# Normalising pair 0 of an attention-and-mixer kernel in a tile of its own, and finishing the first norms on VectorE

## The chip, the cores and the metric

The kernel runs on one core of one Trainium2 chip. The metric is the device time of one launch in microseconds (us); lower is better. A core has TensorE (PE: matrix products and transposes, results in PSUM), VectorE (DVE), ScalarE (ACT), GpSimd (POOL), SyncE (SP, which here only issues transfers), and DMA engines that move data between memory and SBUF. Each engine works through its own list of instructions in order and waits on semaphores for the others.

## The reference

Cosine attention for 8 batches of 12 heads, 448 rows of 64 elements, followed by a mixer over the rows (tokens) and the 768 channels of each batch:

```python
q_n = q / (np.linalg.norm(q, axis=-1, keepdims=True) + 1e-06)
k_n = k / (np.linalg.norm(k, axis=-1, keepdims=True) + 1e-06)
scores = np.matmul(q_n, k_n.transpose(0, 1, 3, 2)) / tau
scores = scores - np.max(scores, axis=-1, keepdims=True)
attn = np.exp(scores)
attn = attn / (np.sum(attn, axis=-1, keepdims=True) + 1e-09)
x = np.matmul(attn, v)            # then heads side by side: [batch, 448, 768]

xt = x.transpose(0, 2, 1)
h = np.maximum(xt @ w_tok1, 0.0) @ w_tok2
u = x + h.transpose(0, 2, 1)
h2 = np.maximum(u @ w_ch1, 0.0) @ w_ch2
out = u + h2
```

`tau` is 0.1. The weights are 448x256, 256x448, 768x1536 and 1536x768.

## The kernel before

**Tiling.** The heads are taken two at a time: 48 pairs, six to a batch. Three pairs make a half batch `n`, whose q, k and v come in one transfer each. The 448 rows of a head are split into 384 main rows, three to each of 128 partitions (`qm`, `km`, `vm`), and 64 rest rows (`xq`, `xk`, `xv`). Rest rows of q lie on 64 partitions, all heads side by side; those of k and v lie on 128 partitions, the two heads of a pair above each other.

**Norms.** For each pair the kernel squares q and k (`squares`, L174 on ScalarE or L176 on VectorE or GpSimd), sums the squares of each row on VectorE (`sums`, L189), and turns sums into reciprocal norms (`rnorms`, L197 to L200: four small ScalarE activations, Ln, Exp with scale 0.5, Ln with the epsilon, Exp with scale -1). `scaled` (L207) multiplies k and q by the reciprocal norm and writes half-precision operands into `kqs`. The rest rows have the same steps, one call for the three pairs of a half batch: `squares_x`, `sums_x` (L193), `scaled_x` (L213 for q, L218 twice for k). Sums and reciprocal norms of a half batch lie in one tile of 45 columns: 0 to 8 for the rest rows, then 12 for each pair.

**A pair.** TensorE transposes the scaled operands into PSUM (`tpose`, L246, L247), VectorE copies them out (`qk_copy`, L251), TensorE computes the scores in three chunks and one for the rest rows (`score`, L266; `score_x`, L273), ScalarE takes the exponential of each (L267, L274), TensorE multiplies by v (`pv`, L287, L289), and VectorE divides by the row sums (L292, L293). `cast_v` brings v to half precision, its main rows on VectorE (L164, for the first two half batches) and its rest rows on GpSimd (L168). Then come the token mixer (L307, L326) and, one whole batch at a time, the channel mixer (L354, L368), whose units are fed between the steps of later pairs.

**Order.** The schedule is written out by hand: each engine runs its instructions in program order. A prologue issues the first loads, fills constants, and carries pair 0 through its norm, with the squares of pairs 1 and 2 placed between. Pair 0's norm runs in two pieces, one for its main rows and one for the rest rows of the whole half batch. `busy` (L232) issues matrix products of no use ahead of and between pair 0's transposes and ahead of the first scores. Then a loop over `i` takes pair `i` through its scores, prepares the norms of later pairs (dictionaries `rn_at`, `sq_at`, `sc_at` say at which `i`), and issues loads on SP's queue. In `i` = 0 GpSimd scales pair 1, issues the token weights on its own queue (L141, L142, L144), scales pair 2, and squares k of pair 3; at `i` = 1 VectorE sums pair 3 and the rest rows of its half batch, and ScalarE starts their norm.

Of the kernel before, what the change touches and what calls it, by code (L numbers as in the profile page):

```python
# [22 lines left out]
def kernel(  # L23
# [56 lines left out]
    sqx = cst.tile([P, 9, E], FP32, name="sqx")  # L80
    ssqs = [cst.tile([P, 45], FP32, name=f"ssq{i}") for i in range(3)]
# [29 lines left out]
    def load_v(n):  # L111
        nc.sync.dma_start(**main(vm, v, "vm", n, bufs=2))

# [69 lines left out]
    def squares_x(n, eq, ek):  # L183
        square(eq, sqx[0:XR, 0:6], xh(xq, n, 6))
        square(ek, sqx[:, 6:9], xh(xk, n, HP))

    def sums(p):
        lo = 9 + 12 * (p % HP)
        nc.vector.tensor_reduce(out=ssqs[p // HP % 3][:, lo:lo + 12],  # L189
                                in_=sq[p][:].rearrange("p a g e -> p (a g) e"), axis=AXX.X, op=ALU.add)  # L190
# [4 lines left out]
    def rnorms(n, c0=0, c1=45):  # L195
        ssq, rn = ssqs[n % 3][:, c0:c1], rns[n % 3][:, c0:c1]
        nc.scalar.activation(out=rn, in_=ssq, func=AF.Ln, bias=tiny[:])  # L197
        nc.scalar.activation(out=rn, in_=rn, func=AF.Exp, scale=0.5)
        nc.scalar.activation(out=rn, in_=rn, func=AF.Ln, bias=eps[:])
        nc.scalar.activation(out=rn, in_=rn, func=AF.Exp, scale=-1.0)  # L200

    def scaled(p, eng):
        n, j = p // HP, p % HP
        for a, src in enumerate((mh(km, p), mh(qm, p))):
            lo = 9 + 12 * j + 6 * (1 - a)
# [4 lines left out]
    def scaled_x(n, eng, j0=0, j1=HP):  # L210
        rn, kq = rns[n % 3], kqs[n % 2]
        gs = slice(2 * j0, 2 * j1)
        eng.tensor_tensor(out=kq[0:XR, j0:j1, 1, NC, :].rearrange("p j (g e) -> p j g e", g=2),  # L213
                          in0=xh(xq, n, 6)[:, gs].rearrange("p (j g) e -> p j g e", g=2),
                          in1=_bcast_free(rn[0:XR, gs].rearrange("p (j g) -> p j g", g=2), E), op=ALU.mult)
        for g in range(2):
            r = slice(XR * g, XR * (g + 1))
            eng.tensor_tensor(out=kq[r, j0:j1, 0, NC, E * g:E * g + E], in0=xh(xk, n, HP)[r, j0:j1],  # L218
                              in1=_bcast_free(rn[r, 6 + j0:6 + j1], E), op=ALU.mult)

# [16 lines left out]
    def tpose(p):  # L237
        n, j = p // HP, p % HP
        pst = ps.tile([P, 8 * P], FP16, name=f"pst_{p}", tag="b")
        if p == 0:  # L240
            w = ps.tile([P, 512], FP32, name="busy", tag="b")
            busy(w, 26)
        for a, c in [(a, c) for a in range(2) for c in range(NC)] + [(0, NC)]:
            if p == 0 and (a, c) == (0, NC):
                busy(w, 4)
            nc.tensor.transpose(pst[:, P * (4 * a + c):P * (4 * a + c + 1)], kqs[n % 2][:, j, a, c], id16[:])  # L246
# [412 lines left out]
```

## Time and profile before

| | |
|---|---|
| median of 9 runs | 415.18 us (413.37 to 416.23) |
| the profiled execution | 413.37 us, of which 411.6 us is the span that the profile covers |
| TensorE busy | 390.7 us, 95% of the span |
| ScalarE | 226.5 us, 55% |
| GpSimd | 213.8 us, 52% |
| VectorE | 201.7 us, 49% |
| mean granted TensorE clock | 0.993 |

The page divides the span into 40 slices of 10.3 us, and gives for each the tenths in which an engine was busy. Further views give the busy time in any stretch, the instructions in order of time, what ended the idle time ahead of an instruction, and the chain of work that ended last. In the timeline a line gives start, duration, engine, line of the program, operation, output and input with shapes, and how many instructions were merged; in brackets stands the idle time before it and what ended that. Names of buffers are given without their numbers.

### The profile page before, as it was taken

Reading aid. Unit: us, or ns where it says so; the run is one execution under the profiler, and the core shown is the slowest. Engines: PE = TensorE matmul, PEld = TensorE weight load, DVE = VectorE, ACT = ScalarE, POOL = GpSimd, SP = SyncE. Lnnn points to the kernel's source line nnn. Section 1 sums busy time; section 2 is a strip of 40 time slices with the busy share of each in tenths; the row PEclk is TensorE's granted clock in tenths of the full one; section 3 lists DMA queues with packets and bytes.
Section 4 is the critical chain, followed back from the end, with each engine's and each line's share of the span. In section 5 each row is a group of like instructions: output and inputs, shape, how many; then the busy total and the mean of one; then the engine's idle time right before and its main releaser. Section 6 shows DMA issues by size and latency. Waiting matters only on the chain.

```text
span 411.6 us, 9121 instructions
## 1 busy us (share of the span) xinstructions
PE 390.7 (95%) x3650; PEld 226.2 (55%) x3650; DVE 201.7 (49%) x455; ACT 226.5 (55%) x405; POOL 213.8 (52%) x314
## 2 busy tenths in 40 slices
PE   8589788999999999999999999999999999999995
PEld 3256444666555655456555555555555565565562
DVE  5588535577543564446543555356553443233021
ACT  4788296974575546664566436664566434611400
POOL 3985669699076675849391937658582500000000
PEclk9989999999999999999999999999999999999998
DMA  7999999989796697969896497979893353013012
GB/s 214 284 241 195 182 244 225 233 201 235 149 224 87 168 196 167 245 127 251 187 246 111 122 222 168 233 115 242 188 184 49 98 136 65 15 53 102 2 76 76
DMA packets 137162, 67.51 MB, mean 164 GB/s; under 512 B 93152, under 2 KB 133536, under 8 KB 137120
## 3 DMA queue, kind: packets, MB, share of 16 engines
q1 hardware_dynamic: 132800, 61.46, 70.6%
q0 software_dynamic: 3632, 5.18, 7.5%
q8 instruction: 28, 0.46, 0.5%
q10 hardware_dynamic: 688, 0.30, 0.3%
q14 instruction: 14, 0.11, 0.1%
HBM read 43.38 MB, written 11.01 MB: 132 GB/s over the span
## 4 chain that ended last, share of the span: by engine, by line
PE 78%; POOL 8%; DVE 5%; issue 4%; ACT 3%; DMA 1%; POOLq 0%; DVEq 0%; ACTq 0%
PE psG L354 25%; PE psF L368 24%; PE psO L287 7%; PE psS L266 7%; PE psR L307 4%; PE psU L326 4%; POOL kq L207 3%; PE psX L273 3%; PE psO L289 2%; POOL sq L176 2%; POOL kq L218 1%; DVE ssq L189 1%; ACT pt L267 1%; DMA km<-in_k_dram 1%; PE psU L331 1%
## 5 line engine op out<-in xcount | busy, mean ns | idle before, releaser
L267 ACT ACTIVATE pt<-psS 128x896 f16<-128x896 f32 x144 | 126.4, 914 | 71.8 <-PE psS L266 71.8
L354 PE MATMUL psG<-ut,wc1t 128*128 128x448 f16 x576 | 122.2, 353 | 0.0
L368 PE MATMUL psF<-wc2t,gt 128*128 128x384 f16 x672 | 117.1, 326 | 0.0
L356 ACT ACTIVATE gt<-psG 128x448 f16<-128x448 f32 x96 | 52.1, 544 | 77.3 <-PE psG L354 77.2
L207 POOL TENSOR_TENSOR kq<-km,rn 128x384 f16<-128x384 f32 x47 | 39.1, 831 | 98.3 <-ACT rn L200 97.1
L368 PEld LDWEIGHTS <-gt 128*128 128x128 f16 x672 | 63.6, 98 | 40.2 <-issue 2.2
L354 PEld LDWEIGHTS <-wc1t 128*128 128x128 f16 x576 | 52.5, 98 | 47.4 <-issue 5.9
L371 DVE TENSOR_TENSOR ost<-psF,ur 128x384 f32<-128x384 f32 x56 | 31.2, 557 | 79.9 <-PE psF L368 78.0
L287 PEld LDWEIGHTS <-pt 128*128 128x128 f16 x1152 | 51.9, 98 | 16.3 <-issue 5.2
L287 PE MATMUL psO<-vt,pt 128*128 128x65 f16 x1152 | 58.0, 194 | 0.0
L189 DVE TENSOR_REDUCE ssq<-sq 128x12 f32<-128x768 f32 x48 | 45.1, 948 | 19.6 <-POOL sq L176 18.4
L266 PE MATMUL psS<-qk 64*128 64x448 f16 x288 | 44.8, 357 | 7.9 <-ACT pt L267 5.5
L176 POOL TENSOR_TENSOR sq<-km 128x384 f32<-128x384 f32 x47 | 39.0, 833 | 9.0 <-DMA km<-in_k_dram 5.6
L293 DVE TENSOR_TENSOR x<-psO,rec 128x256 f16<-128x256 f32 x96 | 40.8, 425 | 3.3
L289 PE MATMUL psO<-vx,pt 128*128 128x130 f16 x192 | 42.0, 219 | 0.0
L207 POOL TENSOR_TENSOR kq<-qm,rn 128x384 f16<-128x384 f32 x47 | 38.9, 828 | 0.0
L292 DVE RECIPROCAL rec<-psO 128x4 f32<-128x4 f32 x96 | 17.1, 178 | 44.5 <-PE psO L289 44.3
L266 PEld LDWEIGHTS <-qk 64*128 64x128 f16 x288 | 11.0, 94 | 38.7 <-issue 32.7
L326 PE MATMUL psU<-w2t,r 128*128 128x448 f16 x96 | 25.9, 353 | 4.2 <-DVE r L310 3.2
L307 PE MATMUL psR<-x,w1t 128*128 128x128 f16 x384 | 29.2, 219 | 0.0
L336 DVE TENSOR_TENSOR ut<-psU,xT 128x448 f16<-128x448 f32 (+2 forms) x39 | 17.6, 477 | 22.5 <-PE psU L326 15.0
L274 ACT ACTIVATE pt<-psX 128x448 f16<-128x448 f32 x48 | 26.0, 542 | 0.0
(62 smaller groups left out, 332.2 us busy)
## 6 DMA issues: line engine op xcount, KB each, us to landing
vm<-in_v_dram SPq DMA_DIRECT2D x16, 576.0 KB, 7.1
out_dram<-ost SPq DMA_DIRECT2D x24, 384.0 KB, 2.8
qm<-in_q_dram SPq DMA_DIRECT2D x15, 576.0 KB, 5.5
km<-in_k_dram SPq DMA_DIRECT2D x15, 576.0 KB, 7.2
wc1t<-in_moe_w_ch_dram POOLq DMA_DIRECT2D x2, 1152.0 KB, 13.5
wc2t<-in_moe_w_ch_dram POOLq DMA_DIRECT2D x2, 1152.0 KB, 12.0
out_dram<-ost SPq DMA_DIRECT2D x8, 192.0 KB, 2.8
xq<-in_q_dram SPq DMA_DIRECT2D x7, 192.0 KB, 7.9
```

Source lines behind the costliest of these rows:

```text
L176: eng.tensor_tensor(out=out, in0=src, in1=src, op=ALU.mult)
L189: nc.vector.tensor_reduce(out=ssqs[p // HP % 3][:, lo:lo + 12], in_=sq[p][:].rearrange("p a g e -> p (a g) e"), axis=AXX.X, op=ALU.add)
L207: eng.tensor_tensor(out=kqs[n % 2][:, j, a, 0:NC, :].rearrange("p c (g e) -> p g c e", g=2), in0=src, in1=_bcast_free(rn, E), op=ALU.mult)
L266: nc.tensor.matmul(psS[:, g, 0:S], qk[r, P * c:P * (c + 1)], qk[r, 512:512 + S], start=True, stop=True)
L267: nc.scalar.activation(out=pt[:, 2 * S * c:2 * S * (c + 1)].rearrange("p (g s) -> p g s", g=2), in_=psS[:, :, 0:S], func=AF.Exp, scale=inv ...
L287: nc.tensor.matmul(psO[:, mm, E1 * g:E1 * (g + 1)], pt[:, at:at + P], vt[:, 2 * j + g, c, 0:E1], start=(g == 0 and c == 0), stop=False)
L289: nc.tensor.matmul(psO[:, mm, :], pt[:, PX + lo:PX + lo + P], vx[:, j, 0:2 * E1], start=False, stop=True)
L307: nc.tensor.matmul(psR[:, tt, :], w1t[:, m, tt * P:(tt + 1) * P], xs[p][:, m, :], start=(m == 0), stop=(m == NC))
L326: nc.tensor.matmul(psU[:], rs[p][:, tt, :], w2t[:, tt, lo:lo + S], start=(tt == 0), stop=by_dma and tt == TT - 1)
L354: nc.tensor.matmul(psG[:], wc1t[:, dt, ct * P:(ct + 1) * P], ut[:, dt, sp], start=(dt == 0), stop=(dt == DT - 1))
L356: nc.scalar.activation(out=gt[:, ct, sp], in_=psG[:], func=AF.Relu)
L368: nc.tensor.matmul(psF[:], gt[:, ct, lo:lo + P], wc2t[:, ct, dh * DH:(dh + 1) * DH], start=(ct == 0), stop=(ct == CT - 1))
```

## The change

- Pair 0's q and k, main rows and rest rows, are loaded into one tile `own` that lies in a buffer of the later tile `ut16`: q as 2 heads of 4 rows (three main, one rest), k as 6 main columns and one rest column. The transfers are q main and q rest on SP, k main and twice k rest on ACT. The unused half of q's rest column is set to zero by VectorE.
- Pair 0 has sums and reciprocal norms of its own. ScalarE squares q, GpSimd k; VectorE reduces each.
- The norm of pairs 0, 1 and 2 is two ScalarE activations (Ln, Exp) and then an add of the epsilon and a reciprocal on VectorE. Pair 1 and the rest rows of pairs 1 and 2 go together; pair 2 follows. Later pairs keep the four activations.
- Pair 0's k is scaled and transposed first, then its q; ScalarE copies the k half out of PSUM and VectorE the q half. Squares of pair 1 and of the rest rows are issued between.
- Pair 1's q half and q's rest rows of pairs 1 and 2 are scaled by VectorE, the k halves by GpSimd; before, VectorE did pair 0's rest rows and GpSimd the others and all of pair 1. These stand in the loop, between the first two score chunks of pair 0, and with them the sum of pair 2.
- The cast of v's first half batch moves from the end of the prologue to behind the token weights' issue; pair 2's scaling follows it.
- The rest rows of k for pairs 1 and 2 are loaded through GpSimd's queue, those of q on SP's queue behind k's load.
- The filler products are 20 and 2 instead of 26 and 4.

```diff
+    own = mix.tile([P, 30, E], FP32, name="own", tag="ut16")
+    q0 = own[:, 0:8].rearrange("p (g c) e -> p g c e", g=2)
+    k0, sq0 = own[:, 8:15], own[:, 15:30]
+    ssq0 = cst.tile([P, 15], FP32, name="ssqp")
+    rn0 = cst.tile([P, 15], FP32, name="rnp")
...
+    def load_pair0():
+        nc.sync.dma_start(out=q0[:, :, 0:NC].rearrange("p g c e -> p g (c e)"),
+                          in_=q[0, 0:2, 0:SM].rearrange("g (p c) e -> p g (c e)", c=NC))
+        nc.scalar.dma_start(out=k0[:, 0:6].rearrange("p (g c) e -> p g (c e)", g=2),
+                            in_=k[0, 0:2, 0:SM].rearrange("g (p c) e -> p g (c e)", c=NC))
+        nc.sync.dma_start(out=q0[0:XR, :, NC], in_=q[0, 0:2, SM:S].rearrange("g p e -> p g e"))
+        for g in range(2):
+            nc.scalar.dma_start(out=k0[XR * g:XR * (g + 1), 6], in_=k[0, g, SM:S])
...
+    def rn_roots(ssq, rn):
         nc.scalar.activation(out=rn, in_=ssq, func=AF.Ln, bias=tiny[:])
         nc.scalar.activation(out=rn, in_=rn, func=AF.Exp, scale=0.5)
+
+    def rn_inverse(rn):
+        nc.vector.tensor_scalar_add(out=rn, in0=rn, scalar1=EPS_NORM)
+        nc.vector.reciprocal(out=rn, in_=rn)
...
+    def scaled_0(part):
+        kq = kqs[0][:, 0, part]
+        if part:
+            nc.vector.tensor_tensor(out=kq.rearrange("p c (g e) -> p g c e", g=2), in0=q0,
+                                    in1=_bcast_free(rn0[:, 0:8].rearrange("p (g c) -> p g c", g=2), E), op=ALU.mult)
+            return
+        nc.vector.tensor_tensor(out=kq[:, 0:NC].rearrange("p c (g e) -> p g c e", g=2),
+                                in0=k0[:, 0:6].rearrange("p (g c) e -> p g c e", g=2),
+                                in1=_bcast_free(rn0[:, 8:14].rearrange("p (g c) -> p g c", g=2), E), op=ALU.mult)
+        for g in range(2):
+            r = slice(XR * g, XR * (g + 1))
+            nc.vector.tensor_scalar_mul(out=kq[r, NC, E * g:E * g + E], in0=k0[r, 6], scalar1=rn0[r, 14:15])
...
-    rn_at = {0: [(0, 33, 45)]}
+    rn_at = {}
...
-        load_q(0, 0, 2)
-        load_k(0, 0, 2, nc.scalar)
-        load_xq(0, 0, 6)
-        load_xk(0, 0, 6, nc.scalar)
+        load_pair0()
         load_q(0, 2, 6)
...
         load_k(0, 2, 6)
+        load_xq(0, 2, 6)
         load_v(0)
...
+        nc.vector.memset(q0[XR:P, :, NC], 0.0)
...
                                 fill=1.0, base=0, pattern=[[-1, P]], channel_multiplier=1)
+        load_xk(0, 2, 6, nc.gpsimd)
...
-        squares(0, nc.scalar, nc.vector)
-        sums(0)
-        rnorms(0, 9, 21)
-        squares_x(0, nc.scalar, nc.vector)
+        w = ps.tile([P, 512], FP32, name="busy", tag="b")
+        busy(w, 20)
+        square(nc.scalar, sq0[:, 0:8], own[:, 0:8])
+        square(nc.gpsimd, sq0[:, 8:15], k0)
+        nc.vector.tensor_reduce(out=ssq0[:, 0:8], in_=sq0[:, 0:8], axis=AXX.X, op=ALU.add)
+        nc.vector.tensor_reduce(out=ssq0[:, 8:15], in_=sq0[:, 8:15], axis=AXX.X, op=ALU.add)
+        rn_roots(ssq0[:], rn0[:])
+        rn_inverse(rn0[:])
+        scaled_0(0)
+        pst = tpose(0, (0,))
         squares(1, nc.scalar, nc.gpsimd)
+        squares_x(0, nc.scalar, nc.gpsimd)
+        scaled_0(1)
+        tpose(0, (1,), pst)
+        nc.scalar.copy(out=qk_tile(0)[:, 0:P * 4], in_=pst[:, 0:P * 4])
+        nc.vector.tensor_copy(out=qks[0][:, P * 4:P * 7 + XR], in_=pst[:, P * 4:P * 7 + XR])
         sums_x(0)
-        scaled(0, nc.vector)
-        rnorms(0, 0, 9)
-        scaled_x(0, nc.vector, 0, 1)
         sums(1)
-        rnorms(0, 21, 33)
+        busy(w, 2)
         squares(2, nc.scalar, nc.gpsimd)
-        scaled_x(0, nc.gpsimd, 1, HP)
-        qk_copy(0, tpose(0))
-        sums(2)
-        cast_v(0)
...
                 score(i, 0, 2 if i < 4 else 0)
+                if i == 0:
+                    rn_roots(*rn_cols(0, 0, 21))
+                    rn_inverse(rn_cols(0, 0, 21)[1])
+                    scaled(1, nc.vector, (1,))
+                    scaled(1, nc.gpsimd, (0,))
+                    scaled_x(0, nc.vector, 1, HP, (1,))
+                    scaled_x(0, nc.gpsimd, 1, HP, (0,))
+                    sums(2)
                 score(i, 1)
...
             if i == 0:
-                scaled(1, nc.gpsimd)
                 weights_tok()
+                rn_roots(*rn_cols(0, 21, 33))
+                cast_v(0)
+                rn_inverse(rn_cols(0, 21, 33)[1])
                 scaled(2, nc.gpsimd)
```

`scaled`, `scaled_x` and `tpose` take a new argument that names the halves (0 for k, 1 for q). `squares_x(0)` leaves pair 0's rest rows out. In half batch 0 the 12 columns of pairs 1 and 2 stand at 9 and 21 (`col`), since pair 0 has its own.

## The prediction

> **What bounds the kernel now.** I read the page's slices first, then a table of busy time by stage, then the chain of work that ended last over the first 80 us, then the timeline of the first 22 us. The slices, one column per 10.3 us:
>
> ```profile
> span 411.6 us, 9121 instructions
> ...
> PE   8589788999999999999999999999999999999995
> ...
> POOL 3985669699076675849391937658582500000000
> ```
>
> TensorE (PE) is full from the eighth slice to the end; the only holes are in the first seven. A change to the start can therefore save only TensorE idle time from before about 70 us. The table by stage (the stretch, its length, busy us and count of PE, of PE's weight loads, of VectorE, ScalarE and GpSimd, then TensorE's granted clock, the DMA engines' share and GB/s) sizes it:
>
> ```profile
> 0.00:10.00 10.00, 8.63 (x34) 3.60 (x35) 5.30 (x15) 4.71 (x12) 3.51 (x18) 1.00 0.77 213
> 10.00:20.00 10.00, 5.48 (x45) 2.40 (x43) 5.75 (x8) 7.07 (x17) 9.06 (x15) 0.99 1.14 280
> 20.00:30.00 10.00, 8.69 (x98) 5.22 (x97) 8.87 (x19) 8.34 (x19) 8.19 (x12) 0.83 1.19 238
> ```
>
> Between 10 and 20 us TensorE works 5.48 us of 10, and the fullest engine is GpSimd (POOL) with 9.06. The chain of waits says the same (start, us, what):
>
> ```profile
> 14.02 1.62 POOL kq L207 x2
> 15.64 0.74 POOL w1t L141
> ...
> 17.65 1.63 POOL kq L207 x2
> 19.28 0.79 POOL sq L176
> ...
> 20.96 0.75 DVE ssq L193
> 21.74 0.32 ACT rn L197
> ```
>
> This is the piece that decides. GpSimd scales pair 1, issues the token weights, scales pair 2, squares pair 3's k; only then can VectorE (DVE) sum pair 3 and ScalarE (ACT) start its norm at 21.74, having sat idle 1.17 us for that sum. On ScalarE this norm stands in front of pair 1's last exponentials, and ScalarE is all but full from there to 29 us. So whatever moves the end of pair 3's square at 20.05 moves all that follows. The timeline shows what stands ahead of it:
>
> ```profile
> 6.81 0.36 DVE L176 TENSOR_TENSOR sqx<-xk 128x192 f32<-128x192 f32 x1 [0.57 <-DMA xk<-in_k_dram]
> ...
> 10.30 1.42 DVE L218 TENSOR_TENSOR kq<-xk,rn 64x64 f16<-64x64 f32 x2
> ...
> 12.53 0.75 POOL L168 CAST vx<-xv 64x192 f16<-64x192 f32 x2
> ...
> 14.02 0.83 POOL L207 TENSOR_TENSOR kq<-km,rn 128x384 f16<-128x384 f32 x1 [0.73 <-ACT rn L200]
> 14.19 1.71 ACT L267 ACTIVATE pt<-psS 128x896 f16<-128x896 f32 x2
> ```
>
> Pair 0's main rows are scaled by 9.54, its rest rows only by the end of the second line, at 11.7; its scores follow and the first exponential starts at 14.19 (last line). Meanwhile GpSimd scales the rest rows of pairs 1 and 2 and casts v's rest rows between 11.02 and 13.28, for nothing, because it waits for pair 1's norm until 14.02 anyway.
>
> **What the Trainium skill says.** "VectorE: DVE Perf Modes" (the TRN2 errata) gives fp32 `tensor_tensor` as (N+151)/0.96 ns: 557 ns for 384 elements, and the trace has 551 to 559. The same page's tier table keeps `tensor_reduce` at one element per cycle; the two reduces here, 948 ns for 768 elements and 750 for 576, differ by 1.03 ns an element. "GPSIMD Engine Reference" (Specifications) says that GpSimd shares its SBUF interfaces with VectorE and contends with VectorE instructions that have two SBUF inputs. The trace agrees: VectorE's 64x64 products of L218 took 565 and 837 ns where the formula gives 224, GpSimd running beside them, and GpSimd's longest square took 1.19 us against a median of 0.82. "TensorE: Matmul & The Clock Gate" (Part 1) says that TensorE falls to half clock after an idle window of about 3.4 us; the trace has a granted clock of 0.83 over 20 to 30 us, and one set of seven transposes spanning 0.95 us there instead of 0.55.
>
> **Part by part: pair 0.** Its q and k with their rest rows now come in five transfers. Pair 0's first sums wait for the rest rows, which they did not before. No row shows a rest transfer this small: from below, q's main rows at 4.14 (issue 0.74 + 3.4); from above, the second xk transfer, whose wait ends at 6.81. The new ones carry 32 KB (q) and 2 x 16 KB (k) instead of 96 and 2 x 48, in the same place of their queues, so a third of the packets: I take 4.9 for both. From there, in us:
> - ScalarE squares q, 512 elements (0.52 plus 128 x 0.83 ns): 5.6. Beside it GpSimd squares k, 448 elements (0.82 plus 64 x 1.68 ns, the slope between its 192- and 384-element rows): 5.9.
> - VectorE reduces q (0.68) and k (0.62): 6.95.
> - Ln and Exp, 0.55 and two hops, as at 6.28: 7.55. Add and reciprocal on VectorE: no such add in the trace; a reciprocal of 128x4 takes 0.178 and a 128x1 memset 0.06, so between 0.2 and 0.4; I take 0.35: 7.9.
> - k scaled (0.55) and its two 64x64 rest pieces, for which I take 0.15 each; from 0.1 to the 0.84 of L218: 8.75. q scaled, 512 elements, 0.69 by the page's formula, plus 0.15 since GpSimd starts pair 1's square near 8.7: 9.6.
> - The q transposes 0.45, the copy of 448 columns 0.4 (0.65 for 960 now): 10.45. k's transposes and ScalarE's copy are done beside this unless the rest rows of q for pairs 1 and 2, queued behind km on SP, land after 9.7; they should be there about 9.2, just after km (seen 8.93 before).
>
> The first scores can thus run from 10.5 instead of 13.32, and the first exponential at 11 instead of 14.19. That gain is large and local: ScalarE would then wait.
>
> **Pairs 1 and 2.** VectorE goes on with the sums of the rest rows (0.76) and of pair 1 (0.95): 12.15. Ln and Exp, which now stand behind the first exponential on ScalarE (11 to 12): 12.75. Add and reciprocal: 13.1. This is when GpSimd may begin pair 1, 0.9 us earlier than 14.02. What it must then do before pair 3's square ends has also changed. Before it was 20.05 - 14.02 = 6.03. Pair 1's q half goes to VectorE: -0.83. The rest rows of k for pairs 1 and 2, hidden before, are now in line: +0.87. The cast of v's rest rows, hidden before, now stands between the weights' issue and pair 2: +0.75. Pair 1's k half runs beside VectorE's q half: as the longest square shows, +0.37 (0 to 0.6). Sum 7.2, so pair 3's square ends at 13.1 + 7.2 = 20.3, against 20.05: **+0.3 us**. The gain on pair 0 is given back on GpSimd.
>
> **The rest of the edits.** The norms of pairs 0 to 2 need 6 small activations instead of 16, 10 x 0.26 = 2.6 us off ScalarE; it costs and brings nothing, since ScalarE waits at 21.74 either way; without that wait it is the second rival. On ScalarE pair 2's roots now wait for VectorE's sum of pair 2, about 15.5, with pair 3's squares and chunk 2's exponential of pair 0 behind them; that exponential comes about 17 to 17.5 instead of 17.65, so no loss. VectorE's order (sum 2, cast of v, inverse, copy of pair 1) puts pair 1's copy at 17 to 18 instead of 16.36; it is hidden by ScalarE, which reaches pair 1 at 18.4 to 18.9, as before (18.87). The xk issues moved to GpSimd's queue cost it two issues of 0.55 to 0.80 around 1.5 to 3, when it only writes constants; by the token weights' 6.6 to 6.9 to landing they are there by 9.8, when GpSimd needs them. The new memset on VectorE could wait for q's transfer if the two are taken to overlap; then 1.5 us of memsets end at 5.7 instead of 2.6, costing 0.1. SP's queue loses one issue and 128 KB ahead of the next loads, about 0.3 us at 350 GB/s, which nothing waits for after 9 us. The fillers on TensorE (20 and 2 for 26 and 4) sit in idle time.
>
> The profiled execution took 413.37 with a span of 411.6; +0.3 gives 413.7 on its terms. The median of the runs is 415.18, so the forecast is 415.5.
>
> **Rivals.**
> 1. *Rest rows late (slower).* If pair 0's rest rows land as the second xk transfer did, 6.75, everything up to pair 3's square slides by 1.85: +2.15, 417.3; half way, +1.2. From a landing of about 5.4 on the loss exceeds 0.83. For it: the first sums did not depend on these rows before, and the DMA engines are at 1.14 of their share in this stretch. Against: a third of the packets, ahead of the big loads.
> 2. *ScalarE was the limit (faster).* If the exponentials, not GpSimd, hold pairs 1 to 3, the 2.6 us taken off ScalarE and the earlier first exponential come through: 412.6; 413.7 if half does. For it: ScalarE is full from 21.74. Against: it idles 1.17 us just before, and the chain runs through POOL.
> 3. *A colder TensorE (slower).* With pair 0 done early, TensorE has little work from about 13 to 15.5; a half clock that reaches past 23 us would double some 2 us of its work on the chain there, about +1 to +2, 416.2 to 417.2. Against: the same happens now from 20 to 23 at no visible cost.
> 4. *The change does not do what it says.* Pair 0 is not earlier because ScalarE's copy waits for late q rest rows; then GpSimd starts pair 1 at 13.5 to 14, and the time is 416 or more. I count it with the first.
>
> **How the numbers follow.** About 0.2% (0.83 us) is what a measurement of this kernel tells from no change. Forecast, between -0.8 and +0.8: 0.40. Slower: rivals 1 and 4 0.26, rival 3 0.09, together 0.35. Faster, rival 2 and savings not seen: 0.25. The unknown costs alone (landing -0.4 to +1.85, contention -0.37 to +0.25, the small VectorE operations -0.3 to +0.8) give 414.3 to 417.3. The range reaches into the faster case to leave a little over 0.1 below it and under 0.1 above: 413.8 to 417.3; the forecast's own range is 414.4 to 416.0.
>
> **What would show it.** Right: first exponential near 11 to 11.5; GpSimd's first product for pair 1 at 13 to 13.5; v's rest cast and the xk products in an unbroken GpSimd run up to pair 3's square, ending 20 to 20.6; ScalarE still waiting for the sum of the rest rows of pair 3. Wrong: a square of `own` starting after 5.4 with a wait on DMA (rival 1), no ScalarE wait before pair 3's norm (rival 2), or doubled matmuls after 23 us (rival 3). An end of pair 3's square below 19.2 would overturn the forecast.

## The result, and the profile after

| | before | after |
|---|---|---|
| median of the runs | 414.94 us (413.37 to 416.49, 32 runs) | 418.79 us (417.14 to 420.42, 10 runs) |
| ratio, 95% interval | | 1.0094 (1.0078 to 1.011) |
| the profiled execution | 413.37 us, span 411.6 us | 419.31 us, span 417.2 us |
| mean granted TensorE clock | 0.993 | 0.979 |

The change costs 3.9 us where 0.3 was forecast. The slices of the kernel after, one column per 10.4 us, show where:

```profile
span 417.2 us, 9106 instructions
...
PE   7579788999999999999999999999999999999995
...
POOL 5787278879439393929293755839391600000000
PEclk9868998999999999999999999999999999999999
```

From the eighth slice on TensorE is as full as before. What differs lies in the first four: its busy share falls from 8 5 8 9 to 7 5 7 9, and the clock row shows it slowed there. The table by stage says so more finely (columns as in the prediction: length; PE, its weight loads, VectorE, ScalarE, GpSimd; granted clock; DMA):

```profile
10.00:20.00 10.00, 4.92 (x28) 1.93 (x29) 7.13 (x13) 6.25 (x13) 7.30 (x10) 0.85 1.06 267
20.00:30.00 10.00, 7.41 (x66) 3.88 (x63) 6.40 (x12) 6.72 (x14) 8.89 (x13) 0.67 1.11 239
30.00:40.00 10.00, 9.55 (x116) 6.55 (x114) 7.17 (x16) 6.71 (x13) 7.85 (x12) 0.79 0.93 198
```

Read the instruction count next to the busy time: from 20 to 30 us TensorE does 66 matrix products in 7.41 us where it did 98 in 8.69, and from 30 to 40 us the granted clock, 1.00 before, is 0.79. GpSimd still has the densest stage, 8.89 us of 10, but it has slid from 10 to 20 us into 20 to 30. The chain of waits passes through it (start, us, what):

```profile
14.82 1.20 POOL kq L239
16.02 1.12 POOL kq L251
...
17.21 0.89 POOL kq L251
18.10 0.35 POOL w1t L156
...
21.59 0.82 POOL kq L239
22.41 0.80 POOL sq L191
...
24.10 0.76 DVE ssq L214
...
24.88 0.32 ACT rn L217
```

The chain has the shape the prediction gave it: GpSimd from pair 1 to pair 3's square, then VectorE's sum, then ScalarE's norm. Its steps come later. GpSimd starts pair 1 at 14.82 (14.02 before), pair 3's square ends at 23.20 (20.05), the norm of pair 3 starts at 24.88 (21.74). The two lines of L251, the rest rows of k, were not in this chain at all before. The timeline shows the steps ahead of it (in brackets the idle time before, and what ended it):

```profile
5.79 0.63 ACT L189 ACTIVATE own<-own 128x512 f32<-128x512 f32 x1 [2.03 <-DMA own<-in_q_dram]
...
8.29 0.17 DVE L221 TENSOR_SCALAR rnp<-rnp 128x15 f32<-128x15 f32 x1 [0.62 <-ACT rnp L218]
8.50 0.25 DVE L222 RECIPROCAL rnp<-rnp 128x15 f32<-128x15 f32 x1
...
11.08 0.59 ACT L546 COPY qk<-pst 128x512 f16<-128x512 f16 x1 [0.30 <-PE pst L291]
...
11.70 0.39 DVE L547 COPY qk<-pst 128x448 f16<-128x448 f16 x1 [1.19 <-ACT qk L546]
...
12.54 0.92 ACT L311 ACTIVATE pt<-psS 128x896 f16<-128x896 f32 x1 [0.45 <-PE psS L310]
...
24.88 0.31 ACT L217 ACTIVATE rn<-ssq,tiny 128x21 f32<-128x21 f32 x1 [2.73 <-DVE ssq L214]
```

First line: the rest rows of q arrive at 5.7. Fourth and fifth: ScalarE's copy of the k half starts after the last q transpose (L291), and VectorE's copy of the q half starts after ScalarE's. The halves are not copied side by side. Sixth: the first exponential is 1.65 us earlier than before (14.19), and the last line shows what that was worth: ScalarE idles 2.73 us for pair 3's sum, instead of 1.17.

Last, TensorE in steps of 2 us, where the third number from the right is the granted clock:

```profile
24.00:26.00 2.00, 0.77 (x12) 0.28 (x8) 1.97 (x6) 1.02 (x5) 1.23 (x2) 1.00 1.30 220
26.00:28.00 2.00, 0.64 (x4) 0.21 (x4) 1.91 (x4) 2.00 (x6) 1.88 (x3) 0.82 1.12 266
28.00:30.00 2.00, 2.00 (x19) 1.08 (x18) 1.75 (x4) 1.97 (x5) 1.93 (x3) 0.50 0.76 152
30.00:32.00 2.00, 2.00 (x19) 1.70 (x18) 0.66 (x1) 1.94 (x5) 1.16 (x3) 0.50 0.99 307
32.00:34.00 2.00, 2.00 (x20) 1.08 (x19) 1.35 (x4) 0.02 (x1) 1.94 (x4) 0.50 0.77 243
```

and the same time in the kernel before:

```profile
24.00:26.00 2.00, 1.13 (x18) 0.80 (x17) 2.00 (x4) 2.00 (x4) 2.00 (x3) 1.00 1.23 225
26.00:28.00 2.00, 1.81 (x26) 1.32 (x25) 1.12 (x5) 1.90 (x6) 1.09 (x3) 1.00 1.15 262
28.00:30.00 2.00, 1.93 (x32) 1.07 (x29) 1.91 (x7) 1.70 (x4) 2.00 (x3) 1.00 1.18 226
```

While the chain waits for pair 3's norm, TensorE has 1.41 us of work in 4. Then its clock falls to half, from 27.3 to 34.1, and for nearly all of this it has all the work that it can do. I call this the second stretch at half clock. The first is there in both kernels, 19.9 to 23.3 before and 17.0 to 23.9 after; it lies almost wholly ahead of the end of pair 3's square, where the chain runs through GpSimd. A third, shorter one comes in the kernel after at 68 to 72 us; before, there is no other in the first 80 us.

**A way to add it up.** Three marks split each span: T, where GpSimd starts its first product of pair 1; Q, where GpSimd ends the square of pair 3's k; G, the start of the first product of the channel mixer (`psG`). In us, after against before:

| | before | after | difference | forecast |
|---|---|---|---|---|
| start to T | 14.02 | 14.82 | +0.80 | -0.9 |
| T to Q, GpSimd's line | 6.03 | 8.38 | +2.35 | +1.2 |
| Q to G | 27.04 | 29.03 | +1.99 | 0 |
| G to the end | 364.5 | 365.0 | +0.5 | 0 |
| span | 411.6 | 417.2 | +5.6 | +0.3 |

This is one execution each. The medians differ by less, 3.9 us. Of the 11 executions of the kernel after whose clock is on record, eight with a mean clock of 0.977 to 0.981 took 419.1 us on average, and three at 0.985 to 0.988 took 418.1: the time at half clock differs from one to the next, and with it the time. Which of the three stretches is missing or shorter in those three, their means do not say.

### The profile page after: what moved, and what is told of

Its sections match the earlier page's. It is cut to its first block, busy times and chain, and to the rows that moved or that the text cites. A ratio compares the mean times of both kernels' runs of the same rounds, so it can differ in the third digit from the quotient of the medians.

```text
span 417.2 us, 9106 instructions
## 1 busy us (share of the span) xinstructions
PE 394.3 (95%) x3642; PEld 227.9 (55%) x3642; DVE 202.9 (49%) x462; ACT 225.3 (54%) x396; POOL 216.3 (52%) x316
## 4 chain that ended last, share of the span: by engine, by line
PE 82%; DVE 6%; POOL 4%; ACT 3%; issue 2%; DMA 2%; SPq 1%; POOLq 0%; ACTq 0%; DVEq 0%
PE psF L412 25%; PE psG L398 25%; PE psO L331 8%; PE psS L310 7%; PE psR L351 5%; PE psU L370 4%; PE psX L317 3%; PE psO L333 2%; POOL kq L251 1%; ACT pt L311 1%; PE pst L289 1%; DMA own<-in_q_dram 1%; DVE ssq L214 1%; DVE x L337 1%; PE psU L375 1%
## 5 line engine op out<-in xcount | busy, mean ns | idle before, releaser
L331 PEld LDWEIGHTS <-pt 128*128 128x128 f16 x1152 | 53.0, 99 | 17.1 <-issue 6.1
L331 PE MATMUL psO<-vt,pt 128*128 128x65 f16 x1152 | 59.1, 196 | 0.0
L210 DVE TENSOR_REDUCE ssq<-sq 128x12 f32<-128x768 f32 x47 | 44.2, 947 | 19.1 <-POOL sq L191 19.0
L351 PE MATMUL psR<-x,w1t 128*128 128x128 f16 x384 | 30.1, 223 | 0.0
## 6 DMA issues: line engine op xcount, KB each, us to landing
wc1t<-in_moe_w_ch_dram POOLq DMA_DIRECT2D x2, 1152.0 KB, 10.4
```

The source lines that it names most:

```text
L331: nc.tensor.matmul(psO[:, mm, E1 * g:E1 * (g + 1)], pt[:, at:at + P], vt[:, 2 * j + g, c, 0:E1], start=(g == 0 and c == 0), stop=False)
L351: nc.tensor.matmul(psR[:, tt, :], w1t[:, m, tt * P:(tt + 1) * P], xs[p][:, m, :], start=(m == 0), stop=(m == NC))
```

## The experiments

My theory after the result: GpSimd's line up to pair 3's square decides, one to one, and the change made it longer and did not start it earlier; a second stretch of TensorE at half clock adds to it. Rivals: pair 0's late rest rows are the whole loss; the norms finished on VectorE are; or the lost time is TensorE's clock alone. Each run was compared with the kernel before on the same chip. All of them in the marks above, in the order run:

| kernel | T | Q | T to Q | Q to G | span | ratio to before (95%) | median less that of before |
|---|---|---|---|---|---|---|---|
| v's cast back in the prologue | 15.69 | 23.19 | 7.50 | 27.2 | 414.8 | 1.0067 (1.0041 to 1.0093) | +2.8 |
| k rest rows on VectorE | 16.47 | 23.24 | 6.77 | 27.2 | 415.8 | 1.0072 (1.0051 to 1.0094) | +3.1 |
| fillers at three places | 15.98 | 24.35 | 8.37 | 27.7 | 418.3 | 1.0116 (1.0093 to 1.014) | +5.0 |
| no rest rows loaded for pair 0 | 15.06 | 23.42 | 8.36 | 28.1 | 416.3 | 1.0089 (1.0066 to 1.0112) | +3.7 |
| first k squares on ScalarE | 14.32 | 22.68 | 8.36 | 28.5 | 416.5 | 1.0103 (1.0085 to 1.0121) | +4.3 |
| four mends together | 14.77 | 21.25 | 6.48 | 27.1 | 413.5 | 1.001 (0.9994 to 1.0027) | +0.6 |
| before, with the longer line | 13.61 | 22.38 | 8.77 | 28.1 | 415.4 | 1.0078 (1.0056 to 1.0099) | +2.8 |
| before, norms finished on VectorE | 13.88 | 19.91 | 6.03 | 27.1 | 412.5 | 0.9998 (0.9978 to 1.0018) | +0.1 |
| fillers at one place | 15.00 | 23.37 | 8.37 | 27.2 | 415.9 | 1.0121 (1.0096 to 1.0146) | +5.4 |
| before, token weights early | 14.64 | 19.55 | 4.91 | 28.1 | 412.0 | 0.9996 (0.9981 to 1.0012) | -0.5 |
| before, pair 1 split | 13.92 | 19.32 | 5.40 | 27.0 | 411.0 | 0.997 (0.9955 to 0.9985) | -1.4 |
| the same, second weight later | 14.04 | 19.43 | 5.39 | 26.9 | 411.6 | 0.9974 (0.9962 to 0.9985) | -1.0 |

Compare the column Q with the last one. Where Q is later than 22 the kernel loses 2.8 us or more; where it is 21.25 or near 20 the kernel is even; where Q is 19.3 to 19.4 it gains. One to one this is not: the marks are of one execution, the last column is of medians, and among the late ones 23.2 goes with +2.8 and 22.7 with +4.3. Every run that moves Q also moves pair 2's scaling, which stands just ahead of it on GpSimd; that the end of this line counts is read from the chain and from ScalarE's wait, not from an experiment.

Q to G tells of the clock. It is 28.1 to 29.0 us in the four executions that have the second stretch (the change and runs 4, 5 and 7), and 26.9 to 27.2 in the others, except run 3 (27.7) and run 10, where another wait came in. So the stretch goes with 1 to 2 us in a profiled execution. It is not the whole loss: runs 1, 2 and 9 do not have it there, and their spans are 3.2 to 4.3 us longer than that of the kernel before.

**1. v's cast back at the end of the prologue** (the kernel after with this edit):

```diff
         squares(2, nc.scalar, nc.gpsimd)
+        cast_v(0, (1,))
...
-                cast_v(0)
+                cast_v(0, (0,))
```

> The changed kernel with one edit: GpSimd's cast of v's rest rows for the first half batch stands at the end of the prologue again (GpSimd waits there from 12.3 to 14.8 us), ahead of pair 1's products; VectorE's part of the cast stays. Theory A (GpSimd's unbroken line from pair 1's products to pair 3's square sets the start, and TensorE's cold time comes on top): pair 3's square ends 0.75 us earlier than 23.2, at about 22.45, and the time is 418.0 against 418.8, ratio to the kernel before 1.007. Theory B (only TensorE's cold stretches cost): no change, 418.8.

GpSimd's line is shorter by 0.88 us. But in this execution T came 0.87 later, and Q did not move; the ratio is 1.0067, next to the expected 1.007. That hit is luck as far as this execution shows, since Q, which was to bring it, did not move; what is missing is the second stretch at half clock. T is late because k of pairs 1 and 2 had arrived by 9.57, so that GpSimd squared it beside VectorE's work on pair 0: the two 64x64 products of L265 took 1.11 us instead of 0.53.

**2. The rest rows of k of pairs 1 and 2 scaled by VectorE** (in the kernel after):

```diff
-                    scaled_x(0, nc.gpsimd, 1, HP, (0,))
+                    scaled_x(0, nc.vector, 1, HP, (0,))
```

> The changed kernel with one edit: the rest rows of k for pairs 1 and 2 are scaled by VectorE (two products of 64x128) instead of GpSimd, where they took 0.89 and 1.14 us. Theory A: GpSimd's line loses 2.0 us, pair 1's transposes come about 1 us earlier, pair 3's square ends at about 21.2, time about 416.8, ratio 1.0045. If contention between the two engines is what stretched these products, VectorE's will be far above the 0.29 us of a free product, and pair 1's GpSimd product stays at 1.2. Theory B: 418.8.

The line is shorter by 1.6 us, the largest single saving, and on VectorE these two products take 0.63 us together. Again T was later, 16.47, and mainly for the same reason: GpSimd's square of pair 1 began at 8.90. Some 0.5 us of it is the landing of pair 0's rest rows of q, which let ScalarE start only at 6.27. The ratio, 1.0072, missed the expected 1.0045.

**3. Fillers on TensorE** before and in pair 1's transposes and ahead of pair 2's scores (in the kernel after):

```diff
+                if p == 1 and a == 0 and c in (0, NC):
+                    busy(fw, 8 if c == 0 else 7)
...
-                score(i, 0, 2 if i < 4 else 0)
+                score(i, 0, 8 if i == 2 else 2 if i < 4 else 0)
```

> The changed kernel with more products of no use on TensorE: 8 ahead of pair 1's transposes and 7 ahead of its last k transpose, where TensorE now waits 1.9 and 1.7 us, and 8 instead of 2 ahead of pair 2's first scores. Theory A: pair 3's square still ends at 23.2, but the granted clock stays near 1 in 27 to 34 us, and the 1.9 us lost there come back: 416.9, ratio 1.005. Theory B (the clock is nearly all of the loss): 415.5 or less, ratio 1.001. If neither the clock nor the time moves, the cold stretch has another cause than the gaps filled here.

It missed. In the profiled execution the second stretch at half clock is gone (clock 1.00 from 22 to 36 us, Q to G 27.7), yet the kernel is no faster, 1.0116: Q came at 24.35, and TensorE was at half clock from 13.5 to 20.3 us and again from 51.0 to 54.4, where the first products of the channel mixer took 0.58 us each instead of 0.35.

**4. No transfers for pair 0's rest rows** (in the kernel after; constants stand in their place, so that this part of the input is left out):

```diff
-        nc.sync.dma_start(out=q0[0:XR, :, NC], in_=q[0, 0:2, SM:S].rearrange("g p e -> p g e"))
-        for g in range(2):
-            nc.scalar.dma_start(out=k0[XR * g:XR * (g + 1), 6], in_=k[0, g, SM:S])
...
-        nc.vector.memset(q0[XR:P, :, NC], 0.0)
+        nc.vector.memset(q0[:, :, NC], 0.1)
+        nc.vector.memset(k0[:, 6], 0.1)
```

> The changed kernel without the three transfers of pair 0's rest rows; the rest rows of pair 0's q and k are set to a constant, so this part of the input is left out. It prices the wait for these rows: squares of pair 0 would start at about 4.2 (q) and 4.7 (k) instead of 5.79. Theory A: all up to pair 3's square is about 1.0 us earlier, time 417.8, ratio 1.007. Theory C (the late rest rows are the main loss): 416 or less, ratio below 1.003. Theory B: 418.8.

Pair 0's Ln starts at 6.64 instead of 7.70, a gain of 1.06 us. All of it is gone before T, and 1.0089 does not differ from the change itself. The timeline of this kernel shows the loss:

```profile
7.21 0.83 POOL L188 TENSOR_TENSOR sq<-km 128x384 f32<-128x384 f32 x1 [1.26 <-DMA km<-in_k_dram]
7.22 0.84 DVE L218 TENSOR_SCALAR rnp<-rnp 128x15 f32<-128x15 f32 x1 [0.62 <-ACT rnp L215]
...
8.36 0.82 POOL L188 TENSOR_TENSOR sq<-km 128x384 f32<-128x384 f32 x1
8.38 1.21 DVE L257 TENSOR_TENSOR kq<-own,rnp 128x384 f16<-128x384 f32 x1
```

VectorE's add of 15 elements, 0.17 us in the kernel after, takes 0.84: it ends when GpSimd's square ends. The product of 384 elements, 0.56, takes 1.21 beside the next square. With fewer small transfers ahead of it k of pair 1 came earlier, and GpSimd's use of it held up VectorE. So dropping these transfers mends nothing; what the late landing alone costs, with k where it was, this run does not say, since it moved k as well. That the landing is the whole loss is ruled out by run 6, where the rest rows come as late (6.0) and the loss is gone, and by run 7, where it is there without them.

**5. The first k squares on ScalarE** (in the kernel after; also the rest rows' squares):

```diff
-        squares(1, nc.scalar, nc.gpsimd)
-        squares_x(0, nc.scalar, nc.gpsimd)
+        squares(1, nc.scalar, nc.scalar)
+        squares_x(0, nc.scalar, nc.scalar)
...
-        squares(2, nc.scalar, nc.gpsimd)
+        squares(2, nc.scalar, nc.scalar)
```

> The changed kernel with the squares of k of pairs 1 and 2 and of their rest rows on ScalarE instead of GpSimd, so that GpSimd does nothing beside VectorE's work on pair 0 from 6.8 us on. Theory A1 (the two engines' contention delays pair 0: VectorE's add, its two 64x64 products and its q product took 0.17 to 0.84, 0.51 to 1.21 and 0.69 to 1.25 us in the runs so far, the high values whenever GpSimd's square of pair 1 had begun): these take 0.17, 0.53 and 0.69, GpSimd's first product of pair 1 starts at 14.4 to 14.9 where the runs so far had 14.8 to 16.0, and the time is about 417.6, ratio 1.007, 1 us below the changed kernel at most. Theory without contention: ScalarE's extra 1.8 us delay its copy of pair 0 and the time is 418.8 or more.

GpSimd is now out of VectorE's way in pair 0, and T is the earliest of these variants of the kernel after, 14.32. The half microsecond against the change itself is the landing of pair 0's rest rows, after which ScalarE starts at 5.28 here and at 5.79 there; in the profiled execution of the change GpSimd's square came too late to stretch VectorE's steps (0.17, 0.53 and 0.69 us, as here). The time is no better: 1.0103. The line is as long as before the edit (8.36), and the second stretch at half clock is there, 29.2 to 32.6 us. A half microsecond at T with an unmended line is not worth anything that shows.

**6. Four mends together** (edits 1, 2 and 5, and one copy out of PSUM for both halves):

```diff
-        nc.scalar.copy(out=qk_tile(0)[:, 0:P * 4], in_=pst[:, 0:P * 4])
-        nc.vector.tensor_copy(out=qks[0][:, P * 4:P * 7 + XR], in_=pst[:, P * 4:P * 7 + XR])
+        qk_copy(0, pst)
```

> The changed kernel with four parts mended together: v's rest cast at the end of the prologue, the rest rows of k for pairs 1 and 2 scaled by VectorE, the squares of pairs 1 and 2 on ScalarE, and one copy of pair 0 out of PSUM by VectorE. Theory A: GpSimd starts pair 1 at about 14.1, its line to the end of pair 3's square is 5.6 us (8.4 less 0.75 and 2.1), so the square ends at about 19.7 against 20.05 in the kernel before; time 414.5, ratio 0.999 (0.996 to 1.003). Theory B (the loss is the clock or pair 0's new order as such): 417 or more, ratio 1.005 and up.

The loss is gone: 1.001 (0.9994 to 1.0027), with the same early pair 0 and the same VectorE norms. GpSimd's timeline shows what it lost and what is late next:

```profile
14.77 1.15 POOL L240 TENSOR_TENSOR kq<-km,rn 128x384 f16<-128x384 f32 x1 [2.38 <-issue]
...
15.86 0.61 POOL L156 DMA_DIRECT2D w1t<-in_moe_w_tok_dram  x1
...
18.85 0.82 POOL L240 TENSOR_TENSOR kq<-km,rn 128x384 f16<-128x384 f32 x1 [1.11 <-DVE rn L223]
...
20.43 0.82 POOL L192 TENSOR_TENSOR sq<-km 128x384 f32<-128x384 f32 x1
```

Behind its first product come the weights at once, with no rest rows and no cast. Then GpSimd idles 1.11 us for pair 2's norm, which passes VectorE behind the cast of v. With the later T (14.77, not 14.1) that is why Q is 21.25 and not the expected 19.7. The run does not tell the four edits apart.

**7. The longer line alone, in the kernel before**: the rest rows of pairs 1 and 2 and v's cast, hidden ahead of T there, go behind pair 1. (The change gave the rest rows of q to VectorE; here they stay on GpSimd.)

```diff
-        scaled_x(0, nc.gpsimd, 1, HP)
...
-        cast_v(0)
+        cast_v(0, (0,))
...
                 scaled(1, nc.gpsimd)
+                scaled_x(0, nc.gpsimd, 1, HP)
                 weights_tok()
+                cast_v(0, (1,))
```

> The kernel before with two pieces of GpSimd's work that its wait hides moved as the change moved them: the rest rows of pairs 1 and 2 are scaled behind pair 1's products, and v's rest rows are cast behind the token weights' issue. Nothing else changes. Theory A: they take 1.45 and 0.75 us there, pair 3's square ends at 22.2 instead of 20.05, and the time is 417.1, ratio 1.005 (1.004 to 1.010 if a cold stretch of TensorE follows). Theory B: GpSimd's place does not matter, ratio 1.000.

1.0078 (1.0056 to 1.0099): pair 0 as it was, ScalarE's norms as they were, and most of the change's loss is there. GpSimd's timeline:

```profile
13.61 0.83 POOL L208 TENSOR_TENSOR kq<-km,rn 128x384 f16<-128x384 f32 x1 [2.75 <-ACT rn L201]
...
15.19 1.13 POOL L214 TENSOR_TENSOR kq<-xq,rn 64x256 f16<-64x256 f32 x1
...
16.29 0.87 POOL L219 TENSOR_TENSOR kq<-xk,rn 64x128 f16<-64x128 f32 x2
...
19.15 0.75 POOL L169 CAST vx<-xv 64x192 f16<-64x192 f32 x2
...
21.56 0.82 POOL L177 TENSOR_TENSOR sq<-km 128x384 f32<-128x384 f32 x1
```

The first line shows 2.75 us of idle GpSimd time that the moved work used to fill; the next ones that it is now paid behind T. Here too TensorE's second stretch at half clock appears (clock 0.57 over 28 to 32 us). So that stretch can follow from a late Q alone, and needs nothing else of the change. Of the medians' 2.8 us, how much is the line and how much the clock was not separated.

**8. VectorE finishes the first half batch's norms, in the kernel before**:

```diff
+        if n == 0:
+            nc.vector.tensor_scalar_add(out=rn, in0=rn, scalar1=EPS_NORM)
+            nc.vector.reciprocal(out=rn, in_=rn)
+            return
```

> The kernel before with one part of the change alone: in the first half batch the add of the epsilon and the reciprocal are done by VectorE instead of ScalarE's second Ln and Exp. Theory A: a norm takes 0.55 + 0.55 us instead of 1.12, GpSimd's start of pair 1 stays at 13.9 to 14.1, and the time is that of the kernel before, ratio 1.000 (0.998 to 1.002). If finishing norms on VectorE is itself a cost, the ratio is above 1.002.

0.9998: this part of the change costs and brings nothing, although T is 0.14 earlier. The interval reaches from -0.2% to +0.2%. The rival that puts the loss on these norms falls.

**9. Fillers only ahead of pair 2's scores** (in the kernel after):

```diff
-                score(i, 0, 2 if i < 4 else 0)
+                score(i, 0, 10 if i == 2 else 2 if i < 4 else 0)
```

> The changed kernel with 10 instead of 2 products of no use ahead of pair 2's first scores, in the gap of 24.8 to 26.0 us that comes before TensorE's second cold stretch, and nowhere else. Theory A: GpSimd's line is as before (pair 3's square ends near 23.2 to 24), the granted clock stays at 1 from 26 to 34 us, the way from that square to the first channel-mixer product is 27.1 to 27.5 us instead of 29.0, and the time is about 417.5, ratio 1.0065, 1.0 to 1.5 below the changed kernel. If the clock falls all the same, or if it stays and the time doesn't fall, the cold stretch is not a cost of its own.

It missed. The profiled execution (417.96 us, mean clock 0.988) had no second stretch at half clock and Q to G at 27.2, as expected. The other five, at 0.973 to 0.981, took 419.4 to 421.6. So the filler is no remedy for the median, and what TensorE's clock alone costs in the median stays open.

**10. The token weights issued in the prologue, in the kernel before**, behind GpSimd's constants:

```diff
         nc.gpsimd.memset(w1t[:, NC, :], 0.0)
+        weights_tok()
...
                 scaled(1, nc.gpsimd)
-                weights_tok()
```

> The kernel before with one edit: GpSimd issues the token weights in the prologue, behind its constants at 3.5 us, where it waits for pair 1's k until 9.0, instead of between pairs 1 and 2. Theory A: 2.0 us leave GpSimd's line, pair 3's square ends at about 18.1 instead of 20.05, and the time is 412.7, ratio 0.995. If the 448 KB delay the loads of q, k and v behind them by more than they spare, pair 1's k lands after 10 us and the ratio is 0.998 or more.

The line shrinks to 4.9 and Q is 19.55, but the ratio is 0.9996, not 0.995. In the timeline:

```profile
15.43 1.42 POOL L207 TENSOR_TENSOR kq<-qm,rn 128x384 f16<-128x384 f32 x1
...
18.75 0.52 ACT L174 ACTIVATE sqx<-xq 64x384 f32<-64x384 f32 x1 [1.26 <-DMA xq<-in_q_dram]
...
22.00 0.31 ACT L197 ACTIVATE rn<-ssq,tiny 128x21 f32<-128x21 f32 x1
```

The next loads came later: the rest rows of q behind the weights took 9.8 us from issue to landing, 7.5 in the kernel before. ScalarE waits 1.26 us for rest rows of q, and pair 3's norm starts at 22.00, later than before (21.74), although Q is earlier. Q decides only as long as nothing else feeds that norm later.

**11. Pair 1 split between the engines, in the kernel before**: the one part of the change that shortens the line, alone.

```diff
-                scaled(1, nc.gpsimd)
+                scaled(1, nc.gpsimd, (0,))
+                scaled(1, nc.vector, (1,))
```

> The kernel before with one part of the change alone: the q half of pair 1 is scaled by VectorE, the k half by GpSimd. Theory (the end of pair 3's k square on GpSimd decides, one to one): GpSimd's line loses a product of 0.8 us and its k product may be stretched by up to 0.4 us beside VectorE's, so the square ends 19.3 to 19.7 instead of 20.05, the norm of pair 3 starts 0.4 to 0.8 us earlier, and the ratio to the kernel before is 0.998 to 0.999. Rival (once that line is shorter, something else sets pair 3's norm, as the rest rows of q did when the token weights were issued early): square ends 19.3 to 19.7, but the norm of pair 3 stays at 21.5 or later and the ratio is 1.000 or more.

0.997 (0.9955 to 0.9985), 413.43 us against 414.79: faster than both kernels, by a little more than expected. The timeline:

```profile
13.92 0.83 POOL L208 TENSOR_TENSOR kq<-km,rn 128x384 f16<-128x384 f32 x1 [0.75 <-ACT rn L200]
...
15.92 0.54 DVE L208 TENSOR_TENSOR kq<-qm,rn 128x384 f16<-128x384 f32 x1
...
18.50 0.82 POOL L176 TENSOR_TENSOR sq<-km 128x384 f32<-128x384 f32 x1
...
20.99 0.31 ACT L197 ACTIVATE rn<-ssq,tiny 128x21 f32<-128x21 f32 x1 [0.52 <-DVE ssq L193]
```

VectorE comes to the q half only at 15.92, while GpSimd issues the weights. So neither product is stretched (0.83 and 0.54; in the change they start together and GpSimd's takes 1.20). Q is 0.73 earlier and pair 3's norm 0.75 earlier, and ScalarE's wait for it falls to 0.52.

**12. The same, and the second token weight's issue behind pair 3's squares**; `weights_tok2` holds the last transfer of `weights_tok` (L144):

```diff
                 norm_begin(p, nc.scalar if p < 18 else nc.gpsimd, nc.gpsimd)
+            if i == 0:
+                weights_tok2()
```

> As the run before, and the issue of the second token weight (0.72 us of GpSimd, ahead of pair 2's scaling) goes behind the squares of pair 3, so that no load is made earlier. Theory: square ends 18.6 to 19.0, 1.0 to 1.4 us ahead of 20.05; ratio 0.9965 to 0.998, better than both kernels. Rival (another wait takes over): the norm of pair 3 at 21.0 or later although the square ends by 19.0, ratio 0.999 to 1.001; or the weights come too late for the token mixer and the loss shows past 40 us.

0.9974 (0.9962 to 0.9985), the same as run 11. The ratio lies in the expected range, but not for the expected reason: Q was to end by 19.0. Freed of 0.7 us of issuing, GpSimd waited 0.81 us for pair 2's norm, and Q stayed at 19.43. So the gain is that of run 11, and the next wait stands right behind the one removed.

## Why the prediction was wrong

**What held.** GpSimd's line up to pair 3's square decides, though not one to one (runs 6, 7 and 11, and the table of experiments). The early first exponential brings nothing, and ScalarE is not the limit: it idles 2.73 us in front of pair 3's norm, so the second rival fell. The only edit costed at nothing that was tried alone, the VectorE norms, cost nothing (run 8). The prediction said that the gain on pair 0 is given back on GpSimd; that is what happened, with three terms too small.

**The start of GpSimd's line: 13.1 forecast, 14.82 measured, 1.7 us.** Two of its steps make up nearly all of it.
- *The landing of the rest rows*, taken as 4.9, was 5.7. The page "DMA: Bandwidth & Descriptors" (Anatomy of one DMA) says, of transfers that GpSimd issues, that they have a fixed part of about 2 us that does not shrink with their size. These were issued by SP, and the trace agrees in kind: q's rest rows, 32 KB, took 4.42 us from issue to landing, and the 96 KB in the same place before had taken 5.0. "A third of the packets" was an argument about the wrong part of the time. In the profiled executions of the change and of runs 1 to 3, 5, 6 and 9 these rows let ScalarE start at 5.3 to 6.3, never at 4.9. This is not quite half of the way to the first rival; run 4, which takes the transfers away, got nothing back.
- *The copies*, taken as side by side, ending 10.45, ended at 12.09, 1.64 late, of which 0.9 was there by the end of q's scaling. The two halves lie in one PSUM tile of 2 KiB, one bank. "PSUM — Partial Sum Buffer" (PSUM bank collisions raise a hardware error) says in its simple form to guard a bank as a whole against any two engines, also where their columns differ. The trace shows just that order: transposes, then ScalarE's 0.59, then VectorE's 0.39. That the bank is the reason, and not the tile being waited for as one piece, no run here separates. With this page the copy of the k half could not have been put beside the q transposes. The fourth rival named ScalarE's copy as the place where the change would not do what it says, because of late rest rows of q. The place was right, and these rows were late: they landed at 10.3 and not at 9.2, and ScalarE was busy with them until 10.78. But what it waited for last, until 11.08, were the q transposes.
- The small VectorE operations, the add (0.17) with the reciprocal (0.25) and the two 64x64 pieces (0.53 for 0.30), add some 0.3.

**GpSimd's line: 7.2 forecast, 8.38 measured.** The whole miss is one term: the two products of k's rest rows, taken from the kernel before at 0.87, took 2.11. The +0.37 for contention was right for the product for which it was taken (1.20 against 0.83), but I gave it to that product alone. Five other runs with the same order show 2.11 again (1, 3, 4, 5 and 9), so it is no chance event. "SBUF — State Buffer" (Who interferes with whom) says that a VectorE instruction with two SBUF inputs, or a copy, cast or tensor_scalar in a two-port mode, contends with GpSimd for ports that one of them holds for a whole instruction while the other waits. Run 4's add, which ended within 0.02 us of GpSimd's square, fits this. The second of the two products fits as well: it ran from 17.21 to 18.10 beside VectorE's cast of v (17.09 to 17.83). For the first (16.02 to 17.14) VectorE's last two-input product ended at 16.30, which explains some 0.3 us of its 0.7 us excess; the rest stays open. Run 2 took the products off GpSimd, and the line was shorter by 1.6 us.

**After pair 3's square: 0 forecast, +2.0 measured in the profile.** I gave the third rival 0.09 and priced it at +1 to +2. Its price was right and its chance too low, but its cause was another: it put the half clock down to TensorE's gap at 13 to 15.5, and what costs is the stretch behind the later gap, 24 to 28. It is not an alternative to the others, as I counted it. It can follow from a late Q, as run 7 shows: the later pair 3's norm, the longer TensorE has next to nothing to do, and then it may run its next work at half clock. "TensorE: Matmul & The Clock Gate" (Part 1) calls the window behind this free-running, so that it varies from run to run. The traces agree. In the first 80 us of each of the fourteen profiled executions the clock changes only at times 3.41 us or a multiple of it apart (in the change it falls at 17.04, 27.28 and 68.24; 10.24 is 3 times 3.41 and 40.96 is 12 times), and where these times lie differs from one execution to the next. Cut into such pieces from 1.4 us on, where the fillers begin, the first 80 us show the clock halved after every piece at full clock with less than 1.65 us of TensorE work, after none with more than 1.95, and after some of those between. In the change the piece from 23.87 to 27.28 held 1.27 us. In run 1 TensorE was nearly as idle (0.65 us of work from 26 to 28 us), but the cuts fell at 23.63 and 27.04, the pieces behind them held 1.91 and 2.10, and it kept its clock. How much of the medians' 3.9 us is due to the stretch stays open: neither attempt to remove it with fillers made the kernel faster (1.0116 and 1.0121, 1.0094 without).

So the step that failed is the sum that ended in "+0.3 us": a gain of 0.9 before the line was set off against a loss of 1.2 in it, with each term taken alone, and nothing was put down for what comes behind. The runs showed a loss of 0.8 before the line, 2.35 in it and 2.0 behind it in the profiled execution. In the line the moved products came to run beside VectorE's work, and the price that I had for them was from a place where only a reduce of VectorE's ran beside them (11.75 to 12.70 before). In front of T the contention itself varies: T was 14.8 to 16.5 in the change and in runs 1 to 3, whose edits lie behind pair 0; in these three runs k of pairs 1 and 2 had arrived earlier (8.9 to 9.6) than in the change (10.09).

## What to carry to other kernels

When work leaves a stretch in which its engine was idle, price it again in the place it goes to, beside what runs there: here 1.6 us that was hidden became 2.9 us on the path. Where two engines work on one PSUM bank, or VectorE and GpSimd work at once, write the order down as a queue before claiming that two steps overlap. And try the parts alone: the one that shortened the deciding line, a few lines of code, gave 0.3% (0.15 to 0.45), while the whole change lost 0.9%.

## What the runs showed of the hardware

- A VectorE instruction of 15 elements took 0.84 us instead of 0.17, ending with a GpSimd product that had started 0.01 us before it (run 4). A price by size misses this.
- VectorE's reduces were not stretched beside GpSimd: 0.94 to 0.95 us for 768 elements in the kernel after (one of them within GpSimd's 2.11 us), and the same in its variants.
- An earlier transfer can make a kernel no faster: run 4's k of pair 1 came at 7.21 instead of 10.09, and GpSimd's use of it took the gain from VectorE.
- TensorE's clock was full or half for pieces of 3.41 us at a time. With 1.27 us of matrix products in such a piece it fell to half and stayed there for 6.8 us of nearly full work (the change); with 1.91 and 2.10 us it did not (run 1). A gap of much the same length can thus leave Q to G at 27.2 us or go with 29.0, by where the pieces begin.
